# Reading eight weight tiles of a delta-rule and MoE kernel with an in-place Prelu and one join

## Chip, cores and metric

The kernel runs on one core of one Trainium2 chip. The metric is device time in microseconds (us), the median of several executions. About 0.5% (3 us) is what a measurement of this kernel can tell from no change.

## The reference, cut to what matters

Two stages follow each other. The first is a delta-rule recurrence over 768 steps for 4 x 8 heads of width 48; the second is a two-layer network on its output, with a Mish activation between the layers. The two weight matrices come as 64-bit floats.

```python
for t in range(S):
    y[:, :, t] = np.einsum('bhd,bhde->bhe', q[:, :, t], state)
    v_old = np.einsum('bhde,bhd->bhe', state, kt)
    state = state + bt[..., None, None] * np.einsum('bhd,bhe->bhde', kt, vt - v_old)
x = y.transpose(0, 2, 1, 3).reshape(B * S, H * D)      # 3072 x 384
h = x @ w_in                                           # w_in 384 x 2048, float64
g = h * np.tanh(softplus(h))                           # Mish
out = (g @ w_out).astype(np.float32)                   # w_out 2048 x 384, float64
```

## The kernel before

**Attention.** The 768 steps are cut into 12 chunks n of 64. A pair of chunks g has a preparation (`early`, L552): k is transposed on DVE (L561), Gram products run on PE (`pg`, L577 and L583), a triangular solve runs as a long chain of small DVE instructions (L712, L713) that ends in the transposes `tu` (L724) and `tt` (L726), and `merge` (L745) joins blocks with the products `ma` and `mb`. Then each chunk runs the product stages `ta`, `tb`, `gq`, `pz`, `py` and `ps` (all issued at L790), with copies on ACT and DVE between them.

**The network.** `moe(n)` (L1128) runs eight blocks for each chunk: `up` (L1144, PE, into `h`), Mish on ACT (L1160, `e`), a copy and a difference that split `e` into a high and a low part (L1161 on ACT, L1162 on DVE), and `down` (L1154, PE, into `acc`).

**The weights.** They lie in 28 tiles, in the order of `parts`: three of `w_in` (`ri`, 128x512 values), four of `w_out` (`ro`, 128x384), and so on. Tile k is loaded as pairs of 32-bit words by SP (L412), and `convert` (L427) makes two fp32r parts of it:

1. ACT scales the high words into a temporary (`scaled`, L452).
2. POOL, for tile 6 DVE, clamps the temporary (L466).
3. POOL writes the sign over the high word (L463).
4. DVE joins the temporary, shifted left by 3, with the sign (L470).
5. DVE joins it with the top three bits of the low word (L470 again; the two joins are told apart by their operands).
6. ACT writes the high part (L482).
7. DVE writes the low part (L493). For the tiles in `LO_PE` two PE products (`loi` and `loo`, L487 and L489) and an ACT instruction (L491) do that instead.

The temporaries are borrowed buffers, named `mi`, `mo`, `spare` and `solved` in the trace. Tile 13 is a `w_out` tile in `spare`; with `LOP` = 13 it is the first tile of `LO_PE`. The load of tile k + `PACE` waits on ACT's scaling of tile k.

**Tables.** `preload_act_table_set` loads ACT's tables: for the square root at the start (L300), then those of Mish right behind the first square root (`guess`, L642 to L647). The second preparation loads the square root's (L645) and then Mish's again (L647).

**What sets the order.** `Plan` (L69) holds every operation with an engine, a duration written in the code and a priority. It plays them through once while the kernel is built, and this fixes the order on each engine. Engines run their instructions strictly in that order. Where the plan sees PE idle before 200 us, it puts filler products there (`warm` and `acc` at L542, `FILL`), and `tiny` adds small ones (`BURN`, `BURN5`; L527). The priorities are the numbers at L1176 to L1190.

```python
copied[k] = o = op("ACT", 0.16 + 0.51 * u, prio, scaled, got, bufs=held)
nc.gpsimd.tensor_scalar(s, a(), 0.0, 1.0, op0=ALU.mult, op1=ALU.mult)          # sign
o = op("DVE", 0.05 + 0.65 * u, prio, lambda: join(words()[:, :, 1], 3, ALU.logical_shift_left), o, bufs=held)
o = op("DVE", 0.05 + 0.65 * u, prio, lambda: join(words()[:, :, 0], 29, ALU.logical_shift_right), o, bufs=held)
```

Of the kernel before, what the change touches and what calls it, by code (L numbers as in the profile page):

```python
# [8 lines left out]
F32 = mybir.dt.float32  # L9
F32R = mybir.dt.float32r  # L10
I32 = mybir.dt.int32
BF16 = mybir.dt.bfloat16
AF = mybir.ActivationFunctionType
ALU = mybir.AluOpType
# [229 lines left out]
def kernel(  # L244
# [182 lines left out]
    def convert(k, got, loads):  # L427
# [16 lines left out]
        def a():  # L444
            return tmp()[:, :n]
# [4 lines left out]

        def scaled():
# [6 lines left out]
        def sign(engine):  # L458
            s = words()[:, :, 1].bitcast(F32)
            if engine == "DVE":  # L460
                nc.vector.tensor_scalar(words()[:, :, 1], words()[:, :, 1], -2 ** 31, None, op0=ALU.bitwise_and)
            else:
                nc.gpsimd.tensor_scalar(s, a(), 0.0, 1.0, op0=ALU.mult, op1=ALU.mult)  # L463

        def clamp(engine):
            engine.tensor_scalar(a(), a(), F64_MOST * 2.0 ** -112, -F64_MOST * 2.0 ** -112, op0=ALU.min, op1=ALU.max)  # L466
# [5 lines left out]
        o = op("POOL", 0.33 + 0.45 * u, prio, lambda: clamp(nc.gpsimd), o, None if k < FIRST else last_s["scaled", 0], bufs=held) if k in CLAMP_POOL else \  # L472
            op("DVE", 0.14 + 0.39 * u, prio, lambda: clamp(nc.vector), o, bufs=held)

        e = "DVE" if k in SIGN_DVE else "POOL"
        o = op(e, 0.13 + 0.38 * u if e == "DVE" else 0.3 + 0.45 * u, prio, lambda: sign(e), o, bufs=held)
        o = op("DVE", 0.05 + 0.65 * u, prio, lambda: join(words()[:, :, 1], 3, ALU.logical_shift_left), o, bufs=held)
        o = op("DVE", 0.05 + 0.65 * u, prio, lambda: join(words()[:, :, 0], 29, ALU.logical_shift_right), o, bufs=held)
# [73 lines left out]
    def early(g, at, gate=None):  # L552
# [136 lines left out]
        if g < ROOTS:  # L689
            o = op("DVE", 0.38, at(0.25), norms, o, last_s.get("root"), bufs=[gr])  # L690
            l = op("DVE", 0.16, at(0.25), least, o)
            o = op("ACT", 2.7 if g else 1.4, at(0.25), guess, o)
# [435 lines left out]
    def moe(n):  # L1128
# [3 lines left out]
        for fp in range(NFP):  # L1132
# [27 lines left out]
            m = op("ACT", 0.58, prio + 0.1, lambda e=e, h=h: nc.scalar.activation(e(), h(), AF.Mish, scale=-1.0), m, bufs=[h, e])  # L1160
# [15 lines left out]
    SOON, SOON1, E1, EG, ES, LATE1, LATE = 0.537, 19.515, -0.143, -0.506, 1.901, -10.483, -1.55  # L1176
    E1S, LAG, PRIO_XT, CV0, CV1, G1A, XA, GQ2 = -1.625, 4.474, 0, -0.235, 0.798, 2.838, -6.856, 4.102
    CC, C1 = (0.225, 0.926, 1.242, 1.418), (5.003, -3.42, -9.481, 1.123)
    VACT, LOP, FIRST, ROOT, LATE_BY = 4, 13, 0, 0.562, 10
    BURN1, BURN2, BURN3, BURN4, BURN5 = 0, 0, 0, 0, 16  # L1180
# [3 lines left out]
    KW, EW, BURN, TQ, PACE = 0, 0, 116, 1, 5  # L1184
    NEAR = 5
# [3 lines left out]
    SIGN_DVE = []  # L1189
# [21 lines left out]
    cvd = {parts[k]: convert(k, got[k], got) for k in range(len(parts))}  # L1211

# [112 lines left out]
```

## Time and profile before

| what | value |
|---|---|
| median of 3 runs | 615.5 us (614.22 to 616.94) |
| the profiled execution | 614.33 us |
| its span, first to last instruction | 612.6 us |
| mean granted clock of PE | 0.983 |
| busy PE / DVE / ACT / POOL | 595.5 / 435.3 / 279.6 / 143.3 us |

The span is what the trace shows; 1.7 us of the execution lie around it. PE is TensorE (its weight loads are PEld), DVE VectorE, ACT ScalarE, POOL GpSimd, SP the engine that issues most DMAs; SPq is its queue. PE's busy time includes filler products. Times inside the span are counted from its first instruction. A clock of 1.00 is 2.4 GHz, 0.50 is 1.2 GHz.

### The profile page before, as it was taken

The page shows a single profiled execution, that of the slowest core. Times are in us where ns is not written, and L with a number is a line of the kernel's source. Part 1 is how long each engine was busy: PE and PEld are TensorE (multiplying, and loading weights), DVE is VectorE, ACT ScalarE, POOL GpSimd, SP SyncE. Part 2 cuts the span into 40 slices and gives each one's busy share as a digit, 9 for nine tenths or more (in the row PEclk, how much of TensorE's full clock was granted, in tenths as well). Part 3 has the DMA queues.
Part 4 walks back from the last instruction along what each step waited for, and adds up shares of the span by engine and source line. Part 5 has one row for each costly group of instructions (what it writes and reads, how often), then busy time and mean ns, then how long its engine had stood idle before and what let it go on. Part 6 is the DMA issues. An engine that isn't in the chain of part 4 may idle for free.

```text
span 612.6 us, 23673 instructions
## 1 busy us (share of the span) xinstructions
PE 595.5 (97%) x10366; PEld 547.7 (89%) x10366; DVE 435.3 (71%) x949; ACT 279.6 (46%) x629; POOL 143.3 (23%) x273
## 2 busy tenths in 40 slices
PE   8989599999999999999999999999999999999997
PEld 4657488899999999999999999999999999999996
DVE  5989989893379988679885798894799874621110
ACT  1846768573643334634236543326533246433231
POOL 6555646100200154010441100441101530000000
PEclk9989679999999999999999999999999999999999
DMA  6989855320133122351143241133131130110011
GB/s 97 259 227 194 196 130 105 54 27 4 31 57 52 40 43 48 54 80 22 25 66 53 44 67 40 20 48 55 36 46 42 37 57 8 23 28 1 2 27 26
DMA packets 158408, 37.81 MB, mean 62 GB/s; under 512 B 151648, under 2 KB 154720, under 8 KB 158304
## 3 DMA queue, kind: packets, MB, share of 16 engines
q1 hardware_dynamic: 153632, 35.85, 30.1%
q8 instruction: 81, 1.33, 0.9%
q10 hardware_dynamic: 4672, 0.44, 0.6%
q14 instruction: 23, 0.19, 0.1%
HBM read 31.56 MB, written 4.72 MB: 59 GB/s over the span
## 4 chain that ended last, share of the span: by engine, by line
PE 92%; DMA 3%; DVE 3%; ACT 1%; issue 1%; SPq 1%; DVEq 0%; ACTq 0%
PE acc L1154 34%; PE h L1144 34%; PE py L790 4%; PE gq L790 3%; PE warm L542 3%; PE pz L790 2%; PE pg L577 2%; PE ps L790 2%; PE tb L790 2%; PE ta L790 2%; PE loo L487 1%; DMA ksrc<-in_k_dram 1%; PE acc L542 1%; DMA qsrc<-in_q_dram 1%; PE loi L487 1%; PE ma L755 1%
## 5 line engine op out<-in xcount | busy, mean ns | idle before, releaser
L1144 PE MATMUL h<-x,wi 128*128 128x256 f32 x1728 | 224.8, 286 | 1.5 <-ACT e L1160 1.3
L1144 PEld LDWEIGHTS h<-x,wi 128*128 128x128 f32 x1728 | 217.6, 193 | 4.5 <-ACT e L1160 1.7
L1154 PE MATMUL acc<-wo,g 128*128 128x384 f32 x1152 | 218.3, 339 | 0.0
L1154 PEld LDWEIGHTS acc<-wo,g 128*128 128x128 f32 x1152 | 196.9, 188 | 3.6 <-issue 0.2
L1162 DVE TENSOR_TENSOR g<-e,g 128x512 fp32r<-128x512 f32 x96 | 66.7, 696 | 104.2 <-ACT g L1161 103.6
L1160 ACT ACTIVATE e<-h 128x512 f32<-128x512 f32 x96 | 57.3, 598 | 146.1 <-PE h L1144 119.7
L1161 ACT CAST g<-e 128x512 fp32r<-128x512 f32 x96 | 59.3, 619 | 82.2 <-PE acc L1154 81.4
L949 POOL TENSOR_SCALAR vt<-vt,ne 128x48 f32<-128x48 f32 x128 | 54.9, 453 | 89.5 <-DVE ne L672 45.0
L713 DVE TENSOR_TENSOR gt<-gt,pr 128x84 f32<-128x84 f32 (+14 forms) x148 | 47.5, 321 | 5.1
L712 DVE TENSOR_TENSOR pr<-gt 128x84 f32<-128x84 f32 (+14 forms) x148 | 47.2, 319 | 3.3
L1007 DVE TENSOR_TENSOR xx<-gq,amask 64x256 f32<-64x256 f32 x88 | 37.1, 422 | 1.6
L606 POOL TENSOR_SCALAR_AFFINE_SELECT d<-at 32x512 f32<-32x512 f32 x20 | 15.2, 762 | 84.0 <-ACT at L597 40.8
L1000 DVE TENSOR_TENSOR vt<-vt,gq 64x192 f32<-64x192 f32 (+1 forms) x66 | 23.3, 353 | 16.0 <-PE gq L790 14.7
L958 DVE STREAM_TRANSPOSE xx<-qsrc 64x512 f32<-64x512 f32 x44 | 31.1, 706 | 2.6 <-PE py L790 1.2
L814 ACT COPY xx<-pz 64x192 f32<-64x192 f32 x92 | 28.8, 313 | 7.9 <-PE pz L790 6.6
L1104 DVE TENSOR_TENSOR xx<-xx,ps 48x192 f32<-48x192 f32 x80 | 28.2, 352 | 2.1 <-PE ps L790 0.6
L790 PE MATMUL gq<-xx,kt 64*64 64x112 f32 (+1 forms) x768 | 29.6, 261 | 0.0
L542 PE MATMUL warm<-zcol,identr 128*128 128x427 f32 (+11 forms) x74 | 28.6, 524 | 0.0
L743 POOL COPY tt<-tt 32x512 f32<-32x512 f32 x24 | 16.3, 679 | 51.7 <-DVE tt L726 26.4
L790 PEld LDWEIGHTS py<-xx 128*32 128x32 f32 (+1 forms) x1536 | 22.2, 106 | 5.3 <-issue 2.7
L790 PE MATMUL pz<-vt,tt 64*64 64x48 f32 x768 | 26.3, 218 | 0.1
L790 PE MATMUL py<-xx 128*32 128x64 f32 (+1 forms) x1536 | 26.2, 220 | 0.0
(150 smaller groups left out, 606.1 us busy)
## 6 DMA issues: line engine op xcount, KB each, us to landing
ri<-in_moe_w_in_dram SPq DMA_DIRECT2D x12, 512.0 KB, 7.1
ro<-in_moe_w_out_dram SPq DMA_DIRECT2D x16, 384.0 KB, 4.8
vt<-in_v_dram SPq DMA_DIRECT2D x24, 192.0 KB, 4.1
xx<-in_k_dram SPq DMA_DIRECT2D x48, 96.0 KB, 3.1
out_dram<-o SPq DMA_DIRECT2D x48, 96.0 KB, 2.2
ksrc<-in_k_dram SPq DMA_DIRECT2D x44, 64.0 KB, 3.1
qsrc<-in_q_dram SPq DMA_DIRECT2D x44, 64.0 KB, 2.5
ksrc<-in_k_dram SPq DMA_DIRECT2D x44, 32.0 KB, 2.5
```

The source lines that it names most:

```text
L542: nc.tensor.matmul(to()[:, 512 - w:], ident, zcol.broadcast_to([P, w]), start=free, stop=free)
L712: nc.vector.tensor_tensor(out=pv, in0=nj, in1=xj, op=ALU.mult)
L713: return nc.vector.tensor_tensor(out=below, in0=below, in1=pv, op=ALU.add).ins
L790: last = nc.tensor.matmul(*a, **flags)
L949: nc.gpsimd.tensor_scalar(vt()[:, p, :], vt()[:, p, :], ne()[:, n16 + p:n16 + p + 1], 1.0, op0=ALU.mult, op1=ALU.mult)
L958: nc.vector.transpose(xx[h][r, :, hh, Q0:K0], src)
L1007: nc.vector.tensor_tensor(out=x[r, p4, hh, Q0:K0], in0=pg[h4]()[i, :, d:], in1=bcast_mid(amask[i], 4), op=ALU.mult)
L1144: nc.tensor.matmul(h()[:, f2, :], wt["i", f * P // WI * NCH + c][:, i2, f0:f0 + P], x[:, c, :], start=(i == 0), stop=(i == 3 * NCH - 1))
L1154: nc.tensor.matmul(acc[t]()[:, :DM], gg()[:, a, f2, ts_], wt["o", f][:, i2, :], start=(f == 0 and i == 0), stop=(f == NF - 1 and i == 2))
L1160: m = op("ACT", 0.58, prio + 0.1, lambda e=e, h=h: nc.scalar.activation(e(), h(), AF.Mish, scale=-1.0), m, bufs=[h, e])
L1161: m = op("ACT", 0.58, prio + 0.1, lambda e=e, gg=gg: nc.scalar.copy(out=gg()[:, 0], in_=e()), m, bufs=[e, gg])
L1162: m = op("DVE", 0.72, prio + 0.1 - PRIO_XT * (n == 1), lambda e=e, gg=gg: nc.vector.tensor_tensor(out=gg()[:, 1], in0=e(), in1=gg()[:, 0], ...
```

## The change

For the first eight tiles (`KP` = 8) ACT's Prelu works in place on the high word: positive values are scaled by 2^-112, negative ones by 2^-80. That puts the sign into an exponent bit, which the later left shift by 3 brings to the place of the sign. The clamp reads the high word and writes the temporary. The sign instruction of POOL goes. The low word is reduced to its top bits ahead of time, by ACT for tiles 0, 1, 2, 4, 5 and 6 and by POOL for tiles 3 and 7. One DVE join is left. The load of Mish's tables moves from behind the first square root to behind the last Prelu, and the Mish instructions wait for it. `LOP` goes from 13 to 14, `PACE` from 5 to 6, `KW` from 0 to 1, `BURN5` from 16 to 0, and the priorities are chosen anew.

```diff
         def scaled():
-            marks[copied[k]] = nc.scalar.activation(a(), words()[:, :, 1].bitcast(F32), AF.Copy, scale=2.0 ** -112).ins
-        copied[k] = o = op("ACT", 0.16 + 0.51 * u, prio, scaled, got, bufs=held)
+            if k < KP:
+                x = nc.scalar.activation(high(), high(), AF.Prelu, scale=2.0 ** -112, alpha=2.0 ** 32)
+            else:
+                x = nc.scalar.activation(a(), high(), AF.Copy, scale=2.0 ** -112)
+            marks[copied[k]] = x.ins
+        copied[k] = o = op("ACT", 0.16 + 0.51 * u, prio + EARLY * (k < KP), scaled, got, bufs=[] if k < KP else held)
...
+        def low(engine):
+            if engine == "ACT":
+                nc.scalar.activation(lows(), lows().bitcast(U32), AF.Copy, scale=0.9375 * 2.0 ** -29)
             else:
+                nc.gpsimd.tensor_scalar(lows(), lows().bitcast(U32), 2.0 ** -29, 7.0, op0=ALU.mult, op1=ALU.min)
...
+        if k < KP:
+            e = "ACT" if k % 4 < LOWA else "POOL"
+            t = op(e, 0.16 + 0.51 * u if e == "ACT" else 0.75 + 1.34 * u, prio + LOWER, lambda: low(e), got)
+            o = op("DVE", 0.05 + 0.65 * u, prio, lambda: join(lows(), 3, ALU.logical_shift_left), o, t, bufs=held)
+        else:
+            o = op("POOL", 0.3 + 0.45 * u, prio, sign, o, bufs=held)
+            o = op("DVE", 0.05 + 0.65 * u, prio, lambda: join(words()[:, :, 1], 3, ALU.logical_shift_left), o, bufs=held)
+            o = op("DVE", 0.05 + 0.65 * u, prio, lambda: join(lows(), 29, ALU.logical_shift_right), o, bufs=held)
...
             nc.scalar.activation(small["y"], small["ss"], AF.Sqrt, scale=0.25)
-            nc.scalar.preload_act_table_set("mish")
+            if g:
+                nc.scalar.preload_act_table_set("mish")
...
-            m = op("ACT", 0.58, prio + 0.1, lambda e=e, h=h: nc.scalar.activation(e(), h(), AF.Mish, scale=-1.0), m, bufs=[h, e])
+            m = op("ACT", 0.58, prio + 0.1, lambda e=e, h=h: nc.scalar.activation(e(), h(), AF.Mish, scale=-1.0), m, *tabled, bufs=[h, e])
...
-    VACT, LOP, FIRST, ROOT, LATE_BY = 4, 13, 0, 0.562, 10
-    BURN1, BURN2, BURN3, BURN4, BURN5 = 0, 0, 0, 0, 16
+    VACT, LOP, FIRST, ROOT, LATE_BY = 4, 14, 0, -0.185, 10
+    BURN1, BURN2, BURN3, BURN4, BURN5 = 0, 0, 0, 0, 0
...
-    KW, EW, BURN, TQ, PACE = 0, 0, 116, 1, 5
+    KW, EW, BURN, TQ, PACE = 1, 0, 116, 1, 6
...
+    KP, LOWA = 8, 3
+    LOWER = 2.821
+    EARLY = 2.816
+    TABLE = -11.132
...
+    tabled.append(op("ACT", 1.28, TABLE, lambda: nc.scalar.preload_act_table_set("mish"), *prelus))
```

## Rows read from the trace of the kernel before

**Rows 1.** The page's 40 slices of 15.3 us: busy tenths of PE and DVE.
```profile
PE   8989599999999999999999999999999999999997
DVE  5989989893379988679885798894799874621110
```

**Rows 2.** Busy time by stretch: from:to, length, engines (x instructions), PE clock, DMA share, GB/s.
```profile
31.00:57.00 26.00, 23.82 (x517) 15.72 (x506) 22.37 (x38) 12.40 (x30) 15.38 (x21) 0.93 0.85 208
57.00:70.00 13.00, 10.40 (x306) 9.69 (x308) 12.62 (x19) 11.87 (x34) 5.11 (x8) 0.75 0.82 157
70.00:98.00 28.00, 23.43 (x365) 18.84 (x357) 25.95 (x41) 20.03 (x44) 16.48 (x21) 0.81 0.73 180
...
31.00:139.40 108.40, 99.05 (x1723) 80.48 (x1715) 97.62 (x179) 73.03 (x180) 44.81 (x61) 0.91 0.60 131
```

**Rows 3.** The chain of waits, 40 to 90 us: start, us, what.
```profile
47.09 1.81 DVE mo L470 x2
...
70.04 1.75 DVE spare L470 x2
...
75.38 1.62 PE loo L487 x2
```

**Rows 4.** Waits of PE, 54 to 91 us: total, times, longest.
```profile
PE loo L487 <- DVE spare L470: 4.6, 1, 4.6
PE h L1144 <- ACT e L1160: 1.3, 1, 1.3
```

**Rows 5.** Timeline of PE and of DVE around 134 us.
```profile
133.75 5.62 PE L542 MATMUL acc<-zcol,identr 128*128 128x128 f32 x48
...
135.81 1.03 DVE L724 STREAM_TRANSPOSE tu<-gt 128x512 f32<-128x512 f32 x1
```

**Rows 6.** Line 470, second joins, 31 to 57 us: ns min/median/max, first and last start.
```profile
L470 DVE SCALAR_TENSOR_TENSOR mi<-ri,mi x3: 685/693/693, 32.6 to 40.6; 128x512 int32<-128x512 int32 x3
...
L470 DVE SCALAR_TENSOR_TENSOR mo<-ro,mo x3: 547/869/926, 43.3 to 51.2; 128x384 int32<-128x384 int32 x3
...
L470 DVE SCALAR_TENSOR_TENSOR spare<-ro,spare x1: 862/862/862, 52.9 to 52.9; 128x384 int32<-128x384 int32 x1
...
L470 DVE SCALAR_TENSOR_TENSOR spare<-ri,spare x1: 674/674/674, 56.0 to 56.0; 128x512 int32<-128x512 int32 x1
```

**Rows 7.** Groups by shape, DVE, 0 to 130 us: busy, mean ns.
```profile
L493 DVE SCALAR_TENSOR_TENSOR wo<-spare,wo 128x384 fp32r<-128x384 f32 x2 | 1.5, 762 | 0.0
```

**Rows 8.** Line 452, 20 to 46 us: ACT's scaling of the high words.
```profile
L452 ACT ACTIVATE mi<-ri x3: 667/688/699, 20.0 to 28.7; 128x512 f32<-128x512 f32 x3
L452 ACT ACTIVATE mo<-ro x3: 542/543/552, 29.2 to 30.1; 128x384 f32<-128x384 f32 x3
```

**Rows 9.** Line 463, 20 to 49 us: POOL's sign instruction.
```profile
L463 POOL TENSOR_SCALAR ri<-mi x3: 651/656/656, 21.6 to 30.9; 128x512 f32<-128x512 f32 x3
L463 POOL TENSOR_SCALAR ro<-mo x3: 727/860/1057, 40.9 to 44.7; 128x384 f32<-128x384 f32 x3
```

**Rows 10.** Waits of POOL, 20 to 57 us.
```profile
POOL tt L743 <- DVE tt L772: 6.9, 1, 6.9
```

**Rows 11.** Timeline of ACT: table load, copies behind it, tile 7's scaling, first Mish.
```profile
15.35 1.28 ACT L647 ACT_TABLE_LOAD   x1
17.35 1.18 ACT L975 COPY xx<-qt 48x512 f32<-48x512 f32 x2 [0.71 <-PE qt L971]
...
35.95 0.65 ACT L452 ACTIVATE spare<-ri 128x512 f32<-128x512 f32 x1
...
64.27 0.60 ACT L1160 ACTIVATE e<-h 128x512 f32<-128x512 f32 x1
```

**Rows 12.** Timeline of DVE: the clamp of tile 6.
```profile
35.23 0.35 DVE L466 TENSOR_SCALAR spare<-spare 128x384 f32<-128x384 f32 x1
```

**Rows 13.** Two stretches of 2 us, columns as in rows 2.
```profile
72.00:74.00 2.00, 0.00 (x0) 0.00 (x0) 1.97 (x4) 1.11 (x3) 1.16 (x3) 0.95 1.08 358
...
82.00:84.00 2.00, 2.00 (x11) 2.00 (x10) 1.94 (x4) 1.43 (x4) 1.30 (x2) 0.50 0.63 73
```

More of the change, by code (lines that the diff above doesn't have):

```diff
@@ L11 @@
 I32 = mybir.dt.int32
+U32 = mybir.dt.uint32
 BF16 = mybir.dt.bfloat16
@@ L448, in words, with clamp, sign @@
             return raw[kind, i].rearrange("p (a b) -> p a b", b=2)
+        high, lows = (lambda: words()[:, :, 1].bitcast(F32)), (lambda: words()[:, :, 0])
         def scaled():
-            marks[copied[k]] = nc.scalar.activation(a(), words()[:, :, 1].bitcast(F32), AF.Copy, scale=2.0 ** -112).ins
-        copied[k] = o = op("ACT", 0.16 + 0.51 * u, prio, scaled, got, bufs=held)
+            if k < KP:
[4 more added lines that the diff above has]
+        copied[k] = o = op("ACT", 0.16 + 0.51 * u, prio + EARLY * (k < KP), scaled, got, bufs=[] if k < KP else held)
         if EW < k < len(parts) - PACE:
             loads[k + PACE].after.append(o)
[L458 to L461, printed above, removed]
-            else:
-                nc.gpsimd.tensor_scalar(s, a(), 0.0, 1.0, op0=ALU.mult, op1=ALU.mult)
-        def clamp(engine):
-            engine.tensor_scalar(a(), a(), F64_MOST * 2.0 ** -112, -F64_MOST * 2.0 ** -112, op0=ALU.min, op1=ALU.max)
+        def clamp(engine):
+            engine.tensor_scalar(a(), high() if k < KP else a(), F64_MOST * 2.0 ** -112, -F64_MOST * 2.0 ** (-80 if k < KP else -112),
+                                 op0=ALU.min, op1=ALU.max)
+        def sign():
+            nc.gpsimd.tensor_scalar(high(), a(), 0.0, 1.0, op0=ALU.mult, op1=ALU.mult)
+        def low(engine):
+            if engine == "ACT":
+                nc.scalar.activation(lows(), lows().bitcast(U32), AF.Copy, scale=0.9375 * 2.0 ** -29)
+            else:
+                nc.gpsimd.tensor_scalar(lows(), lows().bitcast(U32), 2.0 ** -29, 7.0, op0=ALU.mult, op1=ALU.min)
         def join(x, n, f):
@@ L470, in join @@
             return nc.vector.scalar_tensor_tensor(ai, *((ai, n, x) if f == ALU.logical_shift_left else (x, n, ai)), op0=f, op1=ALU.bitwise_or).ins
-        o = op("POOL", 0.33 + 0.45 * u, prio, lambda: clamp(nc.gpsimd), o, None if k < FIRST else last_s["scaled", 0], bufs=held) if k in CLAMP_POOL else \
+        if k < KP:
+            prelus.append(o)
+        held_back = None if k < FIRST else last_s["scaled", 0]
+        o = op("POOL", 0.33 + 0.45 * u, prio, lambda: clamp(nc.gpsimd), o, held_back, bufs=held) if k in CLAMP_POOL else \
             op("DVE", 0.14 + 0.39 * u, prio, lambda: clamp(nc.vector), o, bufs=held)
[L475 to L478, printed above, removed]
+        if k < KP:
+            e = "ACT" if k % 4 < LOWA else "POOL"
[5 more added lines that the diff above has]
+            o = op("DVE", 0.05 + 0.65 * u, prio, lambda: join(lows(), 29, ALU.logical_shift_right), o, bufs=held)
         def first():
@@ L691, in early @@
             l = op("DVE", 0.16, at(0.25), least, o)
-            o = op("ACT", 2.7 if g else 1.4, at(0.25), guess, o)
+            o = op("ACT", 2.7 if g else 0.3, at(0.25), guess, o, *tabled)
+            if g == 0:
+                prelus.append(o)
             last_s.setdefault("guess", o)
@@ L1183 @@
     plan.MARGIN = 1
-    KW, EW, BURN, TQ, PACE = 0, 0, 116, 1, 5
-    NEAR = 5
+    KW, EW, BURN, TQ, PACE = 1, 0, 116, 1, 6
+    NEAR = 4
     plan.LATER = LATE_BY / 10
```

8 lines of the change are left out of this document (4 added, 4 removed).

## The prediction, as put on record

> **What bounds the kernel now.** I first read the busy shares by slice [rows 1]. From the tenth slice to the last but one PE is full: there the time is PE's own work, and a new order of the same work gains nothing. What can be gained lies in the first nine slices, up to about 139 us. DVE's line shows nines and eights in just that part.
>
> Next come the same numbers for chosen stretches [rows 2]. From 31 to 139.4 us DVE is busy 97.6 of 108.4 us, so 10.8 us are idle, 10%. From 57 to 98 us it is busy 38.57 of 41. ACT is at 48% from 31 to 57 us (13.6 us idle) and at 91% from 57 to 70. POOL is at 59% in the first of these stretches.
>
> Then the chain of waits [rows 3]. Between 40 and 90 us it changes among engines, but the pieces on DVE are joins of weight tiles (47.09, 70.04), and the PE piece at 75.38 is the low-part product of a tile. The list of PE's waits puts 4.6 us before that product, released by a join, the longest wait of the stretch [rows 4]. So PE, which works in a fixed order, stands behind DVE's backlog. Last, the end of the stretch [rows 5]: PE runs 48 filler products, 5.62 us from 133.75, while DVE finishes the second solve with `tu` at 136.84. The backlog ends only there. From 31 to 137 us DVE sets the pace, and I cost the change as DVE time.
>
> **What the change takes from DVE.** Eight second joins go. Their rows are 3 x 0.69 = 2.07 us, 0.547 + 0.869 + 0.926 = 2.34 us, 0.86 and 0.67 us, 5.95 us in all [rows 6]. All eight lie between 32.6 and 56.7 us, inside the backlog. `LOP` = 14 moves the low part of tile 13 from PE to DVE, one instruction of 0.76 us [rows 7]. Net 5.2 us.
>
> Not all of it arrives. DVE is idle 10% of that stretch already, waiting for what others deliver, and a shorter queue meets those waits sooner. I take nine tenths: **4.7 us**. The bounds: nothing, if the freed time turns into waits altogether; and above 5.2 us whatever PE recovers by itself, which is priced with the rivals.
>
> **What it adds to ACT.** Six low words. There is no ACT instruction with an unsigned input in this trace; the nearest, ACT's scaling of a word of every pair, takes 0.69 us for 512 and 0.54 for 384 values [rows 8]. Three of each make 3.7 us. The upper bound is the longest elementwise instruction on such a tile, POOL's 1.06 us [rows 9], 6.4 us together; below 3.7 I see no reason to go far, since the sizes are the same. The low words wait only for their load and may be done in ACT's 13.6 idle us up to 57 us. That cover hides either end. If they land after 57 us, where ACT is 91% busy, each microsecond is paid: a rival below. Prelu in place replaces a scaling of the same size, so I add nothing; between nothing and a table load of 1.28 us [rows 11] for each lie the bounds. It needs no temporary and can start when its tile lands.
>
> VectorE's cheap single-source form speaks against using ACT: DVE clamps 384 values in 0.35 us [rows 12], where ACT's scaling takes 0.54. The Trainium skill ("ScalarE: Activation LUTs", Rules for kernel authors) says the same as a rule: give multiplies and minima to VectorE rather than to ScalarE. By that rule the eight low words would cost DVE about 8 x 0.4 = 3.2 us (an estimate from the clamp row), and only 5.2 - 3.2 = 2.0 us would be gained. The sum goes by the engine that has room, so the rule is not followed here.
>
> **POOL.** Eight sign instructions go, about 4 x 0.66 + 4 x 0.86 = 6.1 us [rows 9]. Two low words come. The nearest row is the sign itself, 0.65 to 1.06 us; the duration that the new code plans is far longer, 0.75 + 1.34 u, 1.76 us for tile 3 and 2.09 for tile 7. I take the long one, 3.85 us together, because it is written for just this instruction; POOL is still relieved by 2.2 us. Behind tile 3's low word stand the next clamps. POOL now waits 6.9 us for the attention chain before 38.45 us [rows 10], which covers both. Without that cover, tiles 3 to 5 come up to 1.76 us later.
>
> **The tables.** One load of 1.28 us leaves ACT at 15.35 us. The copies behind it wait for PE anyway, with 0.71 us of idle [rows 11], so nothing is gained. It comes back behind the eighth Prelu. That tile is scaled at 35.95 us now, and the first Mish runs at 64.27; a load in between lies in ACT's idle time. Were the eighth tile late, all Mish instructions would stand behind it, but there are 28 us of slack.
>
> **The rest.** `PACE` = 6 lets SP issue a weight load one scaling earlier; loads move forward past the q, k and v loads in SP's queue, and the stretch moves at 0.85 of DMA time already [rows 2], so I count nothing. Sixteen tiny products go; the plan puts fillers in their place. `KW` = 1 orders two k loads behind one more weight load, some tenths on SP, hidden by the long solve. PE loses two long products of tile 13, which is 1.6 us at the low clock [rows 3], and with them the instruction behind which it stood 4.6 us. What is late next is `ta`, which needs the join of `mb`, again DVE.
>
> **Sum.** The profiled execution takes 614.33 us, with 612.6 of span and 1.7 around it. 614.33 - 4.7 = 609.6. The median shown, 615.5, is 1.2 above the profiled one, so I forecast 609.6 + 1.2 = **610.8 us**, 0.8% faster.
>
> **The rivals.**
>
> *PE's clock comes back too.* In 72 to 74 us PE does nothing, and in 82 to 84 it is busy throughout at a clock of 0.50, the 1.2 GHz level [rows 13]. From 57 to 70 us the granted clock is 0.75 and from 70 to 98 it is 0.81 [rows 2]: 13 x 0.25 + 28 x 0.19 = 8.6 us of full speed are missing. If the waits in front shrink enough to keep the clock, half of this may return, 4 us beyond the forecast: 606.8 us. For it: the wait of 4.6 us hangs on an instruction that is gone. Against: PE would then only reach the second solve sooner, where 5.6 us of filler already stand [rows 5].
>
> The Trainium skill ("TensorE: Matmul & The Clock Gate", The HAM clock gate) has as a rule that the default clock is the lower one and activity releases it; the trace agrees with its 0.50 behind the idle stretch. By that rule this rival and the slower one below are the same mechanism with opposite signs.
>
> *Nothing is gained.* ACT takes DVE's place. It is busy 11.87 of 13 us from 57 to 70 [rows 2], and PE waits there 1.3 us for a Mish [rows 4]. The added 3.7 us and the 1.28 us of the load make 5.0; if the order puts them into this stretch, they cancel the 4.7 us: 615.5 us or so, within 0.5%. For it: the low words have late priorities. Against: they are free of buffers and wait for loads only.
>
> *Slower.* PE's fixed order gains a new long wait. Place: a product behind tile 3 or 7, whose join waits for POOL's low word, or behind a step that the plan thought faster. A wait like today's costs 4.6 us of idle [rows 4], and the clock then stands as from 70 to 98 us, 28 x 0.19 = 5.3 us [rows 2]. 9.9 - 4.7 = 5.2 us slower: 620.7 us. It decides once such a wait passes 4.7 us with its loss of clock. For it: the plan works with constants, and today's order has just such a wait. Against: the fillers were laid out with the same constants and the rest of the order runs within a microsecond.
>
> *The change does not do what it says.* If Prelu's tables were not those loaded for the square root, every Prelu would bring a load and another back, 8 x 2 x 1.28 = 20.5 us on ACT [rows 11], less 13.6 us of idle: about 7 us slower, 622.
>
> **How the numbers follow.** The forecast has 0.44 (its own range 608.5 to 612.5), the clock 0.18, nothing gained 0.22, the new wait 0.13, the tables 0.03. Faster by over 0.5%, so below 612.4 us (about what a measurement of this kernel can tell from no change): 0.42 of the forecast's and 0.18, 0.60. Within 0.5%: 0.02 + 0.22 = 0.24. Slower: 0.16. The range for 8 in 10 reaches from 605, below the clock's 606.8 by its uncertainty, to 618, which leaves out most of the two slower cases, and a little below.
>
> **What would show it.** Right: in 31 to 57 us eight joins fewer on DVE, the wait before the tile product at 75 us gone or short, `tu` of the second solve some 4 to 5 us earlier than 136.84, and from there the same work. The table load should stand before 60 us, and ACT's idle time up to 57 us should fall by about 5 us. Wrong: `tu` no earlier; ACT full from 31 to 70 us with Mish waiting; more than 3 us of new PE idle between 55 and 139 us, or a longer stretch at 0.50; POOL low words far above 2.1 us with joins behind them; more than two table loads before 60 us.

## The result and the profile after

The changed kernel takes **605.67 us** (median of 4 executions, 605.1 to 606.94); the kernel before, measured beside it, 614.86 us (613.63 to 616.94). The ratio is 0.985 with a 95% interval from 0.9817 to 0.9883: 1.5% faster, some 9.2 us. The forecast was 610.8 us, so a gain of 4.7 us. Three single executions below, one of them of the kernel before, took far longer (712, 1723 and 1934 us); they are left out of the ratios, though not of the medians. The time lies inside the range, near its lower end, and the gain is twice the forecast. The profiled execution took 606.05 us, its span 604.3 us, at a mean clock of 0.993.

The page of the changed kernel, engines and slices:

```profile
PE 592.0 (98%) x10341; PEld 542.0 (90%) x10341; DVE 433.3 (72%) x942; ACT 282.3 (47%) x634; POOL 146.1 (24%) x267
...
PE   8989999999999999999999999999999999999996
...
DVE  4898898873399897689895899994898973632110
```

Against [rows 1] PE's fifth slice went from 5 to 9; the five had been the long wait. The stretches of [rows 2] in the changed kernel (columns as there):

```profile
31.00:57.00 26.00, 22.78 (x422) 14.26 (x421) 23.39 (x37) 16.61 (x34) 20.81 (x27) 0.87 0.94 262
57.00:70.00 13.00, 12.20 (x222) 9.48 (x221) 11.46 (x20) 11.71 (x35) 3.89 (x5) 1.00 0.62 127
70.00:98.00 28.00, 26.88 (x574) 22.31 (x574) 26.42 (x44) 22.40 (x52) 15.98 (x24) 1.00 0.67 142
31.00:139.40 108.40, 103.25 (x1891) 83.37 (x1891) 92.31 (x172) 71.95 (x166) 45.52 (x62) 0.97 0.59 131
```

Over the whole stretch DVE is busy 92.31 us where it was 97.62: 5.3 us less, nearly the 5.2 that the prediction counted. (The stretch is fixed in time, so the two hold somewhat different work. Over the whole span DVE is busy only 2.0 us less, 433.30 against 435.30: the differences `g` of the network take 2.9 us more in all, most of them where PE is full.) PE is busy more, not less (103.25 against 99.05), and from 57 to 98 us its granted clock is 1.00 where it was 0.75 and 0.81. The waits of PE up to 140 us (us in total, times, longest):

```profile
PE ta L809 <- DVE tt L791: 2.4, 1, 2.4
...
PE h L1163 <- issue: 0.9, 1, 0.9
PE h L1163 <- ACT x L1136: 0.8, 1, 0.8
PE loi L503 <- DVE solved L480: 0.8, 1, 0.8
...
```

The 4.6 us before tile 13's product [rows 4] are gone. The timeline around the end of the second solve, which answers to [rows 5]; first PE in the kernel before, then PE and DVE in the changed one:

```profile
126.41 2.25 PE L1154 MATMUL acc<-wo,g 128*128 128x384 f32 x12
...
132.82 1.00 PE L790 MATMUL gq<-xx,kt 64*64 64x112 f32 x32
...
139.31 1.26 PE L755 MATMUL ma<-tu,d 16*32 16x16 f32 x128
```

```profile
127.42 2.31 PE L1163 MATMUL h<-x,wi 128*128 128x256 f32 x18
...
129.57 4.40 PE L558 MATMUL acc<-zcol,identr 128*128 128x128 f32 x38
130.22 1.02 DVE L743 STREAM_TRANSPOSE tu<-gt 128x512 f32<-128x512 f32 x1
...
133.90 1.26 PE L774 MATMUL ma<-tu,d 16*32 16x16 f32 x128
```

`tu` ends at 131.24 us instead of 136.84, 5.6 us earlier, and the first `ma` starts at 133.90 instead of 139.31, 5.4 us earlier. In both kernels `ma` starts when the filler ends, 2.5 to 2.7 us behind `tu`. The span shrank by 8.3 us, so 2.9 us more were won somewhere else. They are found by setting the two kernels side by side from the first `ma` to the end. First the kernel before, then the changed one, one stretch each:

```profile
139.31:612.60 473.29, 468.62 (x8041) 450.18 (x8040) 315.71 (x718) 190.07 (x407) 79.82 (x168) 1.00 0.22 38
```

```profile
133.90:604.30 470.40, 465.62 (x8047) 446.36 (x8046) 319.70 (x718) 196.39 (x435) 83.59 (x168) 1.00 0.22 38
```

The clock is 1.00 in both and PE waits for nothing there (0.2 us in the changed kernel) until its work is done, some 4.5 us before the end. What differs is how much work PE has left. PE's groups by shape from the first `ma` on, before and after:

```profile
L1154 PE MATMUL acc<-wo,g 128*128 128x384 f32 x1080 | 204.7, 339 | 0.0
L1144 PE MATMUL h<-x,wi 128*128 128x256 f32 x1548 | 197.8, 284 | 0.0
L790 PE MATMUL gq<-xx,kt 64*64 64x112 f32 x608 | 24.9, 264 | 0.0
```

```profile
L1173 PE MATMUL acc<-wo,g 128*128 128x384 f32 x1068 | 203.0, 338 | 0.0
L1163 PE MATMUL h<-x,wi 128*128 128x256 f32 x1530 | 197.0, 284 | 0.0
L809 PE MATMUL gq<-xx,kt 64*64 64x112 f32 x640 | 26.0, 264 | 0.0
```

Twelve products fewer into `acc` and eighteen fewer into `h`: one whole `down` and one whole `up` are already done when the second solve ends. By the timelines they last 2.25 and 2.31 us. Against them stand one `gq` (1.0 us) that moved behind, and a little more filler: -4.6 + 1.0 + 0.8 = -2.8, nearly the 2.9 us. (The busy times of the groups don't show this sum, since groups overlap: they add up to 526.6 and 525.7 us. PE's busy time of the stretch does: it falls by 3.0, from 468.62 to 465.62 us.)

So the end of this kernel is **the start of the first `ma`, plus the time that PE takes from there**, nearly all of it work. The first term was forecast, the second was taken as unchanged.

The added instructions, by line, in the changed kernel (ns min/median/max, first and last start); the low words on ACT:

```profile
L474 ACT ACTIVATE ri<-ri x3: 640/649/672, 26.2 to 28.5; 128x512 int32<-128x512 uint32 x3
L474 ACT ACTIVATE ro<-ro x3: 538/548/565, 29.9 to 37.0; 128x384 int32<-128x384 uint32 x3
```

the low words on POOL:

```profile
L476 POOL TENSOR_SCALAR ro<-ro x1: 1578/1578/1578, 24.4 to 24.4; 128x384 int32<-128x384 uint32 x1
L476 POOL TENSOR_SCALAR ri<-ri x1: 2184/2184/2184, 37.6 to 37.6; 128x512 int32<-128x512 uint32 x1
```

and the load of Mish's tables and the first Mish in the timeline of ACT:

```profile
56.19 1.28 ACT L1235 ACT_TABLE_LOAD   x1
...
62.35 0.58 ACT L1179 ACTIVATE e<-h 128x512 f32<-128x512 f32 x1
```

### The profile page after: what moved, and what is told of

It reads as the page before. It is cut to its first block, busy times and chain, and to the rows that moved or that the text cites. A ratio compares the mean times of both kernels' runs of the same rounds, so it can differ in the third digit from the quotient of the medians.

```text
span 604.3 us, 23670 instructions
## 1 busy us (share of the span) xinstructions
PE 592.0 (98%) x10341; PEld 542.0 (90%) x10341; DVE 433.3 (72%) x942; ACT 282.3 (47%) x634; POOL 146.1 (24%) x267
## 4 chain that ended last, share of the span: by engine, by line
PE 88%; DVE 5%; ACT 2%; DMA 2%; issue 1%; SPq 1%; ACTq 0%; DVEq 0%
PE h L1163 34%; PE acc L1173 34%; PE py L809 4%; PE gq L809 3%; PE pz L809 2%; PE ps L809 2%; PE pg L593 2%; PE tb L809 1%; PE ta L809 1%; DVE solved L480 1%; DMA ksrc<-in_k_dram 1%; DMA vt<-in_v_dram 1%; PE loi L503 1%; PE loo L503 1%; PE acc L558 1%
## 5 line engine op out<-in xcount | busy, mean ns | idle before, releaser
L1163 PEld LDWEIGHTS h<-x,wi 128*128 128x128 f32 x1728 | 215.0, 190 | 4.9 <-ACT x L1136 1.6
L1181 DVE TENSOR_TENSOR g<-e,g 128x512 fp32r<-128x512 f32 x96 | 69.2, 726 | 86.0 <-ACT g L1180 85.2
L968 POOL TENSOR_SCALAR vt<-vt,ne 128x48 f32<-128x48 f32 x128 | 57.3, 471 | 137.1 <-DVE ne L689 47.7
L558 PE MATMUL warm<-zcol,identr 128*128 128x433 f32 (+12 forms) x74 | 30.7, 551 | 0.0
```

The source lines that it names most:

```text
L558: nc.tensor.matmul(to()[:, 512 - w:], ident, zcol.broadcast_to([P, w]), start=free, stop=free)
L968: nc.gpsimd.tensor_scalar(vt()[:, p, :], vt()[:, p, :], ne()[:, n16 + p:n16 + p + 1], 1.0, op0=ALU.mult, op1=ALU.mult)
L1163: nc.tensor.matmul(h()[:, f2, :], wt["i", f * P // WI * NCH + c][:, i2, f0:f0 + P], x[:, c, :], start=(i == 0), stop=(i == 3 * NCH - 1))
L1181: m = op("DVE", 0.72, prio + 0.1 - PRIO_XT * (n == 1), lambda e=e, gg=gg: nc.vector.tensor_tensor(out=gg()[:, 1], in0=e(), in1=gg()[:, 0], ...
```

## The experiments

The theory after the result: DVE's shorter queue gives some 4 to 5 us, and the re-chosen order gives as much again. Differences between the runs of under 3 us rest on their traces more than on their medians. Rivals were that the numbers alone do it, that PE's clock does it, and that only the length of the filler differs. In some runs every engine's order is that of the kernel before or of the changed kernel, and single instructions are taken out or put in; in others the plan is played again, and the order shifts with the edit. The text says which. The kernel before ran beside all of them, with medians from 614.0 to 614.6 us.

### New numbers, old reading

The changed kernel with no tile read in the new way; the plan is played again.

```diff
-    KP, LOWA = 8, 3
+    KP, LOWA = 0, 3
```

> The changed kernel with KP = 0: all new numbers and the order made from them stay, but all 28 tiles are read the old way. Theory (the eight joins taken off DVE are the cause): DVE gets its 5.3 us back, the second solve's tu ends at 135 to 138 us instead of 131.2, PE stalls and loses clock between 57 and 98 us again, time 612 to 617 us. Rival (the new numbers and LOP = 14 are the cause): 605 to 608 us, and the clock from 57 to 98 us stays at 1.00.

Measured: 622.65 us (620.85 to 624.48), ratio 1.0134, interval 1.0107 to 1.016. That is 8.6 us slower than before, outside both expectations, though the clock from 57 to 98 us is as good as in the changed kernel. Stretches, then PE around the second solve:

```profile
57.00:70.00 13.00, 11.65 (x363) 9.06 (x364) 11.39 (x21) 11.11 (x34) 3.40 (x7) 1.00 0.60 128
70.00:98.00 28.00, 27.58 (x374) 22.32 (x374) 24.89 (x44) 23.76 (x53) 13.81 (x20) 1.00 0.68 165
```

```profile
133.34 6.42 PE L558 MATMUL acc<-zcol,identr 128*128 128x128 f32 x56
139.51 2.33 PE L1173 MATMUL acc<-wo,g 128*128 128x384 f32 x12
141.77 1.38 PE L774 MATMUL ma<-tu,d 16*32 16x16 f32 x128
```

PE works at full clock, but fills: 6.42 us here and more later, 14.3 us of `acc` filler against 5.9 us in the changed kernel. From `ma` to the end it is 480.9 us, where the changed kernel has 470.4, and in 10.1 us of it PE is not busy (4.8 there). The new numbers are not better in themselves.

### Old numbers, new reading

The changed kernel with all numbers of the kernel before; the plan is played again (the diff shows two of the seven lines).

```diff
-    VACT, LOP, FIRST, ROOT, LATE_BY = 4, 14, 0, -0.185, 10
+    VACT, LOP, FIRST, ROOT, LATE_BY = 4, 13, 0, 0.562, 10
...
-    KW, EW, BURN, TQ, PACE = 1, 0, 116, 1, 6
+    KW, EW, BURN, TQ, PACE = 0, 0, 116, 1, 5
```

> The changed kernel with the numbers of before (LOP 13, PACE 5, KW 0, BURN5 16, the old priorities), but with the new reading of eight tiles. Theory (joins): most of the gain is there, 606 to 610 us. Rival (numbers): 613 to 616 us.

Measured: 618.49 us (617.93 to 619.3), ratio 1.0067, interval 1.0049 to 1.0084: 4.5 us slower than before, which neither theory nor rival expected. PE's longest wait up to 140 us, and two stretches:

```profile
PE loo L503 <- DVE spare L480: 5.8, 1, 5.8
```

```profile
57.00:70.00 13.00, 6.51 (x306) 5.95 (x306) 12.37 (x24) 11.65 (x32) 4.37 (x7) 0.78 0.64 138
70.00:98.00 28.00, 25.20 (x281) 19.56 (x282) 20.06 (x32) 19.28 (x44) 15.44 (x21) 0.80 0.69 169
```

DVE is busy 6.2 us less over the long stretch (91.43 against 97.62 us), and yet PE waits 5.8 us before the same product, and DVE itself stands idle 8 of 28 us behind it. `ma` starts at 136.54 us, 2.8 earlier than before, but from there to the end it is 479.7 us, 6.4 more: here one `up` and one `down` more are left (1566 and 1092 products), and PE's busy time from `ma` on is 5.3 us longer. So neither half of the change gains when the plan is played again with it; both together do.

### Tile 13's low part on DVE, alone

The kernel before with `LOP` = 14; the plan is played again.

```diff
-    VACT, LOP, FIRST, ROOT, LATE_BY = 4, 13, 0, 0.562, 10
+    VACT, LOP, FIRST, ROOT, LATE_BY = 4, 14, 0, 0.562, 10
```

> The kernel before with LOP = 14 alone: tile 13's low part goes from PE to DVE, and with it the product behind which PE stood 4.6 us. Theory (joins): DVE has 0.76 us more to do and its backlog only makes PE wait elsewhere; 613 to 616 us. Rival (that one product in PE's fixed order is the cause): the wait is gone and nothing takes its place, clock above 0.9 from 70 to 98 us, 607 to 611 us.

Measured: 615.2 us (10 executions), ratio 1.002, interval 0.9997 to 1.0042: no change that can be told, as the theory had it. The wait of 4.6 us is gone and one of 3.0 us for ACT stands in its place; the clock stays at 0.75 and 0.81.

```profile
PE loi L487 <- ACT at L597: 3.0, 1, 3.0
```

### Filler in front of tile 13's product

The kernel before, orders kept, with six products put where PE waits, so that the clock stays up.

```diff
+            def one():
+                for _ in range(6 if k == 13 else 0):
+                    nc.tensor.matmul(ps()[:, :n], ident, zcol.broadcast_to([P, n]), start=True, stop=True)
...
```

> The kernel before with six filler products of 384 columns on PE ahead of tile 13's low-part product, about 3.9 us in the wait of 4.6 us; no other work changes. Theory (clock gives half of it): the clock from 74 to 84 us is 1.00 instead of 0.50, the products there are done about 4 us sooner, and the time is 610 to 612.5 us. Rival (only DVE's backlog counts): the clock comes back but tu of the second solve stays near 136.8 us and the time at 614 to 616 us.

Measured: 614.1 us (10 executions), ratio 0.9988, interval 0.9966 to 1.001: no change. Stretches and PE's timeline:

```profile
57.00:70.00 13.00, 10.65 (x244) 9.74 (x243) 12.63 (x21) 11.07 (x35) 4.14 (x6) 0.82 0.81 144
70.00:98.00 28.00, 26.14 (x435) 19.63 (x435) 27.39 (x42) 21.25 (x46) 18.26 (x24) 0.96 0.82 200
```

```profile
134.29 5.62 PE L547 MATMUL acc<-zcol,identr 128*128 128x128 f32 x48
139.85 1.26 PE L760 MATMUL ma<-tu,d 16*32 16x16 f32 x128
```

The clock from 70 to 98 us rose from 0.81 to 0.96, and `ma` starts no earlier, as the rival had it. In the order of the kernel before, this much of the clock by itself is worth nothing that can be measured.

### Eight DVE instructions put back into the changed kernel

Orders kept; behind each of the eight joins DVE runs a second one of the same shape.

```diff
+            def twice():
+                join(lows(), 3, ALU.logical_shift_left)
+                w1 = words()[:, :, 1]
+                nc.vector.scalar_tensor_tensor(w1, w1, 3, a().bitcast(I32), op0=ALU.logical_shift_left, op1=ALU.bitwise_or)
...
```

> The changed kernel in its own order, with one more DVE instruction behind each of the eight joins, of a second join's shape, writing into a word that nothing reads any more; the plan's durations stay, so no engine's order changes. Theory (the order is right and DVE's time sets the pace): tu of the second solve 5 to 6 us later than 131.2, PE waits of some us between 60 and 98 us, time 610 to 614 us. Rival (the order alone brings the gain; the joins' time matters little): 605 to 608 us.

Measured: 609.86 us (608.94 to 613.15), ratio 0.9947, interval 0.992 to 0.9974. That is 4.2 us over the changed kernel and 4.4 us under the kernel before, between the two expectations. The eight instructions take 5.65 us on DVE. PE's timeline in three places:

```profile
43.96 1.97 PE L814 MATMUL ta<-tt,at 32*64 32x64 f32 x32 [6.47 <-DVE tt L796]
...
133.28 4.40 PE L563 MATMUL acc<-zcol,identr 128*128 128x128 f32 x38
137.61 1.26 PE L779 MATMUL ma<-tu,d 16*32 16x16 f32 x128
```

The wait before the first `ta`, ahead of 43.96 us and not between 60 and 98 us as expected, grows from 2.4 to 6.5 us, and everything behind it, `ma` too, is some 4 us late. The clock from 57 to 98 us stays at 1.00. From `ma` to the end it is 608.1 - 137.61 = 470.5 us, as in the changed kernel. In the new order, then, DVE's time shifts `ma` and leaves the rest as it is. What still sets this run apart from the kernel before is the order together with the rest of the new reading (POOL's eight signs gone, six low words on ACT and two on POOL); the run without joins and signs, below, helps to part them.

### The kernel before without the second joins

Orders kept.

```diff
-        o = op("DVE", 0.05 + 0.65 * u, prio, lambda: join(words()[:, :, 0], 29, ALU.logical_shift_right), o, bufs=held)
+        o = op("DVE", 0.05 + 0.65 * u, prio, lambda: join(words()[:, :, 0], 29, ALU.logical_shift_right) if k >= 8 else None, o, bufs=held)
```

> The kernel before in its own order, leaving out the second join of the first eight tiles, so the three lowest bits of their single-precision values are missing. Theory (DVE's time): the 4.6 us wait before tile 13 shrinks, tu of the second solve ends at 131 to 133 us, time 607 to 611 us. Rival (the removed time only pays in an order made for it, as the run with old numbers and new reading suggests): 612 to 615 us, with DVE waiting longer for others.

Measured: 611.6 us (609.02 to 617.34, 10 executions), ratio 0.9977, interval 0.9946 to 1.0009. The median is 2.6 us lower, between the two expectations, but the executions scatter, and the interval takes in no change. The profiled execution was the longest of them (617.34 us), so nothing is read from its trace.

### The kernel before without second joins and signs

As the last, and POOL's sign instruction of the first eight tiles is left out too, so the kernel leaves out work that the output needs.

```diff
-        o = op(e, 0.13 + 0.38 * u if e == "DVE" else 0.3 + 0.45 * u, prio, lambda: sign(e), o, bufs=held)
+        o = op(e, 0.13 + 0.38 * u if e == "DVE" else 0.3 + 0.45 * u, prio, lambda: sign(e) if k >= 8 else None, o, bufs=held)
...
```

> As the run without second joins, and also without the POOL sign instruction of the first eight tiles, so their first join merges the raw high word. If POOL's relief counts beside DVE's: 2 us or more below that run. If it does not: within 1.5 us of it.

Measured: 610.25 us (608.66 to 612.95, 10 executions), ratio 0.994, interval 0.9917 to 0.9962: 4.0 us faster. With the instructions gone and the old order kept, the gain is what the prediction took from DVE's rows, 4.7 us, a little less. The median is 1.35 us below that of the last run, within the 1.5 us that were to say that POOL's relief does not count; with the scatter of that run this decides little. The trace shows more than the time:

```profile
133.27 1.26 PE L755 MATMUL ma<-tu,d 16*32 16x16 f32 x128
```

`tu` ends at 130.8 us and `ma` starts 6.0 us earlier than before, more than in the changed kernel, and 2.0 of them are lost behind `ma`: from there to the end it is 608.6 - 133.27 = 475.3 us, against 473.3. The work left is the same, product for product; up to 160 us PE stands idle 1.8 us, in several short waits that the profile puts down to nothing ("issue").

### Old numbers, new reading, tile 13 on DVE

As the second run, with `LOP` = 14; the plan is played again.

```diff
-    VACT, LOP, FIRST, ROOT, LATE_BY = 4, 13, 0, 0.562, 10
+    VACT, LOP, FIRST, ROOT, LATE_BY = 4, 14, 0, 0.562, 10
```

> The new reading with the old numbers and LOP = 14 alone changed. Theory (the one product of tile 13 in PE's order is what kept the new reading from paying, 5.8 us of wait with the old numbers): 608 to 612 us. Rival (all numbers have to fit together): 614 to 619 us.

Measured: 613.52 us (610.72 to 617.19, 10 executions), ratio 0.9989, interval 0.996 to 1.0019. The same number that did nothing alone takes off 5.0 us here, and the time falls between the two expectations. `tu` ends at 129.40 us, even earlier than in the changed kernel, and still the time is 7.9 us longer: PE runs filler for 5.85 us from 126.33, which outlasts `tu`, and has more work left. (The trace is of the fastest execution, 610.72 us, so it accounts for 4.7 us of the 7.9.)

### Ten fillers fewer in the changed kernel

Orders kept. The changed kernel's filler ends 2.7 us behind `tu`. (`stops` counts the places where the plan puts filler; each product shows twice in the profile.)

```diff
-        for _ in range(n):
+        for _ in range(n - 10 if len(stops) == 14 else n):
```

> The changed kernel with every engine's order kept, and one thing taken out: of the 19 filler products (38 recorded) that PE runs from 129.57 us while DVE ends the second solve, 10 are left out, so that 9 remain (about 2.1 us instead of 4.40). In the changed kernel tu ends at 131.24 and PE's filler at 133.97, so PE outlasts tu by 2.7 us. Theory A (from tu on PE is the bound, and filler that outlasts the solve is paid in full): ma starts about 2 us earlier and the whole is 1.8 to 2.4 us shorter, 603.3 to 603.9 if the changed kernel gives 605.7. Rival B (what follows waits for POOL's clearing of ym, for ACT and for DVE anyway, so PE's filler hides a wait): ma starts earlier, mb or a later stage waits as much longer, and the time stays within 0.6 us of 605.7. Rival C: the shorter filler costs PE its clock behind 131 us; the time rises by more than 1 us and the granted clock from 131 to 150 us falls under 0.95.

Measured: 603.76 us, ratio 0.9818, interval 0.9789 to 0.9848: 1.9 us under the changed kernel, as theory A had it. Nothing is read from its trace; the run with twelve fillers fewer, below, shows the same cut in one.

### Eleven fillers fewer in the kernel before

Orders kept; the same edit at the filler of [rows 5].

```diff
-        for _ in range(n):
+        for _ in range(n - 11 if len(stops) == 13 else n):
```

> The kernel before with every engine's order kept; of the 24 filler products (48 recorded, 5.62 us from 133.75) 11 are left out, 13 remain (about 3 us, to 136.8, where tu ends at 136.84). Theory A (filler that outlasts the solve is paid in full): 2.0 to 2.6 us shorter, 612 if the kernel before gives 614.3. Rival B (the filler hides a wait for ym, ACT or DVE): within 0.8 us of 614.3. This also says what of the gain of the changed kernel was only in the filler's length: 1.2 us of it (5.62 against 4.40) by theory A, nothing by B.

Measured: 611.42 us, ratio 0.9963, interval 0.9935 to 0.9991. The medians differ by 3.2 us, the ratio says 2.3 (0.4%), where theory A had 2.0 to 2.6. From `ma` to the end it is 608.8 - 134.99 = 473.8 us, as before. In this trace `tu` itself ends 2.0 us earlier, at 134.84, and `ma` starts 0.15 us behind it. Filler that outlasts the solve is paid nearly in full in both kernels, so it does not tell them apart.

### The changed kernel without its fillers from 53 to 63 us

Orders kept.

```diff
-        for _ in range(n):
+        for _ in range(0 if len(stops) in (11, 12, 13) else n):
```

> The changed kernel with every engine's order kept, without its fillers of 53.60, 58.59 and 60.09 us (4.72 us of products that write nothing the output needs). Behind each of them PE waits for another engine, so the time of those waits is not PE's to give. Theory A (the half of the gain that DVE's time does not explain is PE's clock, kept at 1.00 from 57 to 98 us): the clock in 57 to 98 us falls to 0.75 to 0.9, and the whole is 2 to 5 us longer, 608 to 611. Rival B (the clock in that stretch is worth nothing, because DVE's solve sets the end of it, as in the kernel before with filler ahead of tile 13): the clock falls as much, and the time stays within 1 us of 605.7. If the clock stays above 0.97, the run says nothing on either, and then the fillers themselves were not needed there.

Measured: 606.65 us (606.16 to 607.77), ratio 0.9875, interval 0.9837 to 0.9912. One of the stretches, and PE at the second solve:

```profile
57.00:70.00 13.00, 10.96 (x201) 9.16 (x200) 10.40 (x17) 9.17 (x30) 2.60 (x4) 0.69 0.66 135
```

```profile
130.03 4.41 PE L558 MATMUL acc<-zcol,identr 128*128 128x128 f32 x38
134.37 1.26 PE L774 MATMUL ma<-tu,d 16*32 16x16 f32 x128
```

The clock from 57 to 70 us fell to 0.69, lower than before the change, and the time rose by 1.0 us. `ma` starts 0.5 us later, and what is left is the same, 604.4 - 134.37 = 470.0 us. From 70 to 98 us the clock stayed at 1.00, so the expectation's fall did not come over the whole stretch. Where it came, 13 x 0.31 = 4.0 us of full speed were lost, and 4.7 us of filler were spared, of which the two waits there took back 3.1 us (for `h` 2.7 instead of 0.8, for `loi` 2.0 instead of 0.8). The time speaks for rival B; but the slower clock of the kernel before from 70 to 98 us, the larger part, is not brought back here, so what the new order would lose by it is not shown.

### Tile 13 back on PE in the changed kernel

`LOP` = 13 and nothing else; the plan is played again.

```diff
-    VACT, LOP, FIRST, ROOT, LATE_BY = 4, 14, 0, -0.185, 10
+    VACT, LOP, FIRST, ROOT, LATE_BY = 4, 13, 0, -0.185, 10
```

> The changed kernel with LOP = 13 instead of 14, all other numbers kept; the plan is played again, so the order shifts. Theory A (order and durations were chosen together; tile 13's product on PE brings back a wait for its join): a PE wait of over 2 us at tile 13's product or behind it, the clock in 57 to 98 us below 0.95, and 609 to 612. Rival B (only the work moves: 0.76 us off DVE, about 1.1 us of products onto PE): 605.5 to 607, clock 1.00.

Measured: 609.01 us (606.73 to 609.62), ratio 0.99, interval 0.9866 to 0.9935: 3.3 us slower than the changed kernel, more than the 1 us of moved work. The clock stays at 1.00, which the first theory did not expect although its time came; no wait of over 2 us is new. `tu` ends at 131.9 us, and the order puts a `down` between the filler and `ma`, which then starts at 136.87. From there it is 470.0 us, only 0.4 less than in the changed kernel, although one `down` less is left: the count of products gives the rest within some 2 us, not exactly.

### Twelve fillers fewer, for the trace

The changed kernel, orders kept, 7 of 19 fillers left.

```diff
-        for _ in range(n):
+        for _ in range(n - 12 if len(stops) == 14 else n):
```

> The changed kernel, every order kept, with 12 of the 19 fillers at 129.57 us left out, so 7 remain (about 1.6 us of recorded time instead of 4.40, a little less than the solve lasts). Theory A (from ma on PE runs without a wait to the end, so the time is the start of ma plus PE's remaining work): ma starts 2.4 to 2.8 us earlier, at about 131.3 instead of 133.90; from ma to the end of the span it stays 470.4 us; 603.0 to 603.6 in all. Rival B (what follows waits for POOL, ACT or DVE): ma starts as early, but PE shows over 1 us of waits between 131 and 200 us, and from ma to the end over 471.5 us.

Measured: 603.04 us (600.9 to 604.24), ratio 0.9817, interval 0.979 to 0.9844: 2.6 us under the changed kernel. PE's timeline, and the stretch from `ma` to the end:

```profile
127.47 1.73 PE L558 MATMUL acc<-zcol,identr 128*128 128x128 f32 x14
129.29 1.25 PE L774 MATMUL ma<-tu,d 16*32 16x16 f32 x128
```

```profile
129.29:599.20 469.91, 465.24 (x8046) 446.20 (x8046) 322.24 (x724) 198.19 (x440) 83.93 (x169) 1.00 0.22 39
```

No wait of PE is listed behind 125 us. The profiled execution is the fastest of the five (600.9 us; in it `tu` ends at 129.1 us, which the edit doesn't touch), but the stretch behind `ma` is what counts, and it is as long as in the changed kernel, as theory A had it. This version is faster than the kernel before; against the changed kernel it was not run side by side, but the executions of the two do not overlap.

### Old numbers, new reading, tile 13 on DVE, twelve fillers fewer

Orders kept against the eighth run.

```diff
-        for _ in range(n):
+        for _ in range(n - 12 if len(stops) == 13 else n):
```

> The old numbers with the new reading and LOP = 14 (613.5 us, filler from 126.33 to 132.1 us, tu at 129.46), every order kept, with 12 of the 25 fillers left out, 13 remaining (3.0 us). Theory A (an early end of the solve is lost where PE's filler outlasts it, and the rest of the distance to the changed kernel is PE work not yet done at that point): 2.4 to 2.9 us shorter, 610.6 to 611.1, still 5 us over the changed kernel, with PE's remaining work from the end of the filler at 477 us against 470.4. Rival B (the fillers' length is the only thing that the new numbers set right): 605 to 608.

Measured: 611.66 us (609.43 to 614.77, 10 executions), ratio 0.9954, interval 0.9929 to 0.998: 1.9 us less than with the long filler, and still 6.0 us over the changed kernel. PE at the second solve:

```profile
127.78 3.17 PE L558 MATMUL acc<-zcol,identr 128*128 128x128 f32 x26
132.08 2.41 PE L1163 MATMUL h<-x,wi 128*128 128x256 f32 x18 [1.13 <-ACT e L1179]
134.43 1.26 PE L774 MATMUL ma<-tu,d 16*32 16x16 f32 x128
```

Behind the filler PE now waits 1.1 us for a Mish, which the first theory had not counted; the rest of it came. From 132.08 us it is 610.1 - 132.08 = 478.0 us to the end, 7.6 us more than the changed kernel has from its `ma`. By the groups of the trace about half of it is work not done ahead (one `up` and one `down` more, one `gq` less, 3.6 us); 2.6 us are more filler behind `ma`, and 1.2 us more idle time of PE. So the length of the filler at the solve is not the only thing that the new numbers set right, as rival B would have it.

## Why the prediction was right and wrong

The gain has two terms when the runs are put beside each other. Each row keeps one order; the columns differ in DVE's work:

| order | with eight more joins on DVE | without them |
|---|---|---|
| of the kernel before | 614.0 to 614.6 us (before itself) | 611.6 us; 610.25 without signs too |
| of the changed kernel | 609.86 us | 605.67 us (the change itself) |

Downwards is the order's worth, 4.4 us with the joins (614.23 measured beside that run); to the right is DVE's worth, 4.2 us in the new order and 2.6 to 4.0 in the old. The step downwards also takes in what the new reading does on POOL and ACT; where both kernels lack joins and signs it is 4.6 us (610.25 to 605.67), so POOL's signs are not what gives it. Added up the two make 8.6 of the 9.2 us; the kernel before itself had medians from 614.0 to 614.9 in the several comparisons. In the traces the gain divides into the start of the first `ma` and the rest of the span; in the last three rows the plan was played again:

| run | first `ma` | from there to the end |
|---|---|---|
| before | 139.31 | 473.3 |
| before, filler before tile 13 | 139.85 | 473.7 |
| before, eleven fillers fewer | 134.99 | 473.8 |
| before, without joins and signs | 133.27 | 475.3 |
| after, eight joins more | 137.61 | 470.5 |
| after | 133.90 | 470.4 |
| after, without early fillers | 134.37 | 470.0 |
| after, twelve fillers fewer | 129.29 | 469.9 |
| after, tile 13 on PE | 136.87 | 470.0 |
| old numbers, new reading | 136.54 | 479.7 |
| new numbers, old reading | 141.77 | 480.9 |

**What the change takes from DVE: right.** 5.2 us net were counted, 5.3 are missing from DVE's busy time. Nine tenths, 4.7 us, were to arrive. With the order held, 4.2 us arrive in the new order and 4.0 in the old one (for the eight joins alone, without tile 13's 0.76 us, and in the old one without POOL's signs too). That the two agree is in part luck: in the new order the whole shift of `ma` arrives, in the old one `ma` comes 6.0 us earlier and loses 2.0 behind; `tu` came 5.6 us earlier, where "some 4 to 5" were expected. One reading was short: `ma` does not wait for `tu` alone, but for the end of PE's filler 2.5 us behind it, and cutting that filler took off 1.9 to 2.6 us.

**"From there the same work": wrong.** This is the step that failed. The prediction took from rows 1 that behind the ninth slice "a new order of the same work gains nothing". It costed `PACE`, `BURN5` and `KW` one by one, found each small or hidden ("I count nothing"), and gave the re-chosen priorities, and `NEAR` (another number of the plan, from 5 to 4), no term at all; of PE's recovered time it said that "PE would then only reach the second solve sooner, where 5.6 us of filler already stand". That sentence holds for an order that is kept: with filler in front of tile 13 most of the clock came back and nothing was gained. But the changed kernel's order is played anew, and the plan puts one more `up` and one more `down` where PE is free ahead of the solve. The term was put at nothing and measures 4.4 us. The traces have 4.5: a rest shorter by 2.8 (473.3 to 470.5), and `ma` earlier by 1.7 at nearly equal DVE work (139.31 to 137.61). Without the joins they have 4.3, divided otherwise: a rest shorter by 4.9 (475.3 to 470.4; PE is busy 3.4 us less in it and idle 1.5 us less), and `ma` later by 0.6. What makes that idle time, and what moves `ma` by 1.7, stays open.

**The rival "PE's clock comes back too": near in time, not the cause by itself.** It gave 606.8 us, and the clock did come back. But the run that regained most of it in the old order gained nothing, the run with the new numbers and the old reading had full clock and was the slowest of all, and the run that lost the clock from 57 to 70 us again (0.69) was only 1.0 us slower, spared 4.7 us of filler. Full clock and no long wait make room on PE (it is busy 4.2 us more from 31 to 139.4 us); in these runs the room became time only where the order filled it with work. Whether the new order would keep its gain at the old clock from 70 to 98 us no run shows.

**"Nothing is gained": did not come.** ACT is as busy from 57 to 70 us as before (11.71 us), and PE's waits for Mish are gone from the list.

**"Slower": a real mechanism, in another kernel.** The new reading under the old numbers has just this wait, 5.8 us before the product of a tile, with clocks of 0.78 and 0.80 behind it. It was priced at 620.7 us and measured 618.49. The new numbers are what kept the change out of it.

**Tables: right.** Between the load at the start and the second preparation there is one, at 56.19 us, 4.9 us ahead of the first Mish, counted from its end; the Prelus (0.54 to 0.67 us) bring none.

**The additions on ACT and POOL: right.** The six low words take 0.54 to 0.67 us, as the scaling row said, and lie between 26 and 38 us; ACT's idle time from 31 to 57 us fell by 4.2 us, and up to 57 us by 4.6, where about 5 were expected. The low words on POOL take 1.58 and 2.18 us, close to the code's 1.76 and 2.09 that were taken, and nobody is listed as waiting for them. The Trainium skill ("ScalarE: Activation LUTs", Rules for kernel authors) would have multiplies and minima like these on VectorE. No run puts the low words there, so the rule itself is not tested. What the runs show for a full DVE is that eight more instructions on it, 5.65 us of larger ones, cost 4.2 us, while for the six on ACT, 3.6 us, only a wait of 0.6 us is listed.

What stays open is which of the re-chosen numbers lets the plan do the `up` and the `down` ahead. Tile 13's place alone is not it: moving it to DVE gave +1, -5.0 and -3.3 us in three settings.

## What to carry to other kernels

Where an order is made by playing a plan, a change of durations and a change of the plan's numbers have no price of their own: here each alone, with the plan played again, lost (4.5 and 8.6 us), and both together gained 9.2, while with the order held the removed instructions alone gave 4.0 us. When one engine is full to the end, cost a change in two terms, when that engine's unbroken run starts and how much of its work and waiting is left then; ask of every recovered idle stretch whether the order can put real work there. And look for filler that outlasts the wait it covers: cutting it gave about 2 to 3 us in either kernel, the smallest edit of this study that gained.

## What was not expected of the hardware

On POOL the same reduction of a word, from unsigned to signed 32-bit integers, takes 1.58 us for 384 and 2.18 us for 512 values a partition, where the sign instruction of [rows 9] takes 0.86 and 0.66 us (medians); on ACT it takes 0.55 and 0.65 us, no more than ACT's scaling of a float. And filler that held PE's clock among waits was worth little here: 4.7 us of it taken out, the clock down to 0.69 for 13 us, and 1.0 us lost; in the old order the clock raised from 0.81 to 0.96 for 28 us, and nothing gained.
